# Attention scores in a fused attention and feed-forward kernel: q and k split into high and low parts, three float32r products per head pair in place of plain float32 tiles

## The chip, the cores and the metric

The kernel runs on one core of a Trainium2 chip. The metric is the device time of one launch in microseconds (us), as the median of several runs. TensorE (PE) does matrix products; its weight loads are listed as PEld. VectorE is DVE, ScalarE is ACT, GpSimd is POOL, and SyncE (SP) issues the DMAs. Each engine runs its own instructions in the order in which they were written.

## What is computed

```python
q, k, v: (4, 12, 448, 64); w_pre, w_post: (12, 12)
scores = scale * np.matmul(q, k.transpose(0, 1, 3, 2))
scores = np.einsum('bhij,hg->bgij', scores, w_pre)
scores = scores - np.max(scores, axis=-1, keepdims=True)
attn = np.exp(scores)
attn = attn / (np.sum(attn, axis=-1, keepdims=True) + 1e-09)
attn = np.einsum('bhij,hg->bgij', attn, w_post)
attn_out = np.matmul(attn, v)
# x: (4, 448, 768), the heads side by side
h = x.transpose(0, 2, 1) @ U @ V
u = x + h.transpose(0, 2, 1)
out = u + np.maximum(u @ w_ch1, 0.0) @ w_ch2      # 768 -> 3072 -> 768
```

All inputs and the output are float32.

## The kernel before

The work has three stages. In the first, attention runs over 16 units (4 batches, 4 groups of rows each) and 180 chunks of 10 rows. In the second, the products with w_ch1 run (`product`, L970), and in the third those with w_ch2 (`down`, L1078). Both of these use float32r operands that are kept as a high and a low part, with three products (low by high, high by low, high by high) summed in one bank.

The first stage goes through these steps.

- **Scores** (`qk`, L402 to L409): for each unit and each of 6 head pairs p, 96 times in all, four plain float32 products of 64 rows by 64 (or 60) columns. A pair's two heads lie in rows 0 to 63 and 64 to 127 of q and k; the 124 query columns are cut in two halves. One line of the program becomes two matrix instructions, so that a pair has 8.
- **Relay** (`qk_out` L411, `relay` L415): a copy of 124x896 from the bank to the tile s (three buffers), on ACT or DVE, and two DMAs from s to the tile t, which turn the layout round. The head mix needs all 12 relays of its unit.
- **Head mix and softmax**: `premix` (L440, 8 instructions), the maximum on DVE (L447), the exponentials on ACT (L452), `add_eps` on POOL (L455), the reciprocal on DVE (L458), `scale_w` on POOL (L462), and `postmix` (L476, 56 instructions). These two products too are of 64 rows by 64 columns.
- **Values** (`av`): 36 instructions at L517 of 128 rows by 64 columns, and 24 at L525 of 64 by 64. The path through U and V (L729, L746, L760) uses all 128 by 128.

The order is not left to a scheduler at compile time: `Plan` holds every step with a rank (the table `RANK`), engines it may run on with planned costs, and the slots of the buffers it needs, and plays the program through; what comes out is written to the engines in that order. Four PSUM tiles of two banks are shared by all steps.

Two more parts are touched. `narrow` turns float64 words of w_ch1, U and V into float32 with chains of DVE and POOL instructions; 11 such pieces ("early" ones) run within the first stage, through the raw tiles `kr`. At the start POOL sets parts of both t tiles to zero (L379).

Of the kernel before, what the change touches and what calls it, by code (L numbers as in the profile page):

```python
# [22 lines left out]
NG = 4  # L23
# [22 lines left out]
class Unit:  # L46
# [10 lines left out]
RANK = dict(  # L57
    e0=-75.527, estep=7.598, er=5.082, qk_lead=5.047, qk_step=0.838, av_off=4.137, av_step=0.9, post=4.408,
    kr=1.361, vr=0.943, qr=5.087, mx=0.654, ex=1.029, ep=2.968, po=2.286, qo=0.493, uv0=6, uvs=0.155, uv1=2.315,
    raw=5.531, k0=-13.668, kstep=0.83, m0=7.671, pu=1.842, ev=29.543, lead=14.78, t0=-2.958, ts=0.557, t1=2.815,  # L60
    ta=37.05, tb=3.706, dl=32.545, hl=13.674, out=3,
)
# [182 lines left out]
def build(tc, q2, kt, vj, wpre_in, wpost_in, u_in, v_in, ident, w1j, w2, out, show=None):  # L245
# [5 lines left out]
    def pool(ctx, name, bufs, side="left", **kw):  # L251
# [3 lines left out]
    BUFS = dict(  # L255
        wr=3, e=3, st=4, a0=1, a1=1, vr=1, kr=2, k=2, q=3, s=3, x=2, ea=1, xn=1, t3=1, hs=10, hr=5, b0=1, b1=1, b2=1,
    )
# [27 lines left out]
    pool(t0_ctx, "t0", 1)  # L285
    for n in ("kr", "x", "ea"):
        pool(whole, n, BUFS[n], "right")
    uT = [[None] * 7 for _ in range(2)]
# [8 lines left out]
    open_uT(0, 0)  # L297
    for n in ("k", "q", "s"):
        pool(qk_ctx, n, BUFS[n], "right")
# [89 lines left out]

    def load_k(eng, b, p, n):  # L390
        k = tile_of(("k", b), lambda: sb["k"].tile([128, H // 2, S], F32, "k", ("k", b)))
        eng.dma_start(out=k[:, p:p + n], in_=kt[b, :, p:p + n])

    def load_q(eng, u, p, n, src):
        q = tile_of(("q", u), lambda: sb["q"].tile([128, H // 2, QW], F32, "q", ("q", u)))
        eng.dma_start(out=q[:, p:p + n], in_=src[:, p:p + n])

    for b in range(B):
        for p, n in ((0, 1), (1, 2), (3, 3)):
            plan.add(("k", b, p), [("SP", (450, 1050 * n))], partial(load_k, b=b, p=p, n=n), rank_qk(b * NG, 2 * p) - RANK["kr"], (), [("k", b)])  # L400
# [18 lines left out]
    for u, un in enumerate(units):  # L419
        b, size = un.b, 128 * (H // 2) * QW  # L420
        src = q2[at:at + size].rearrange("(p h i) -> p h i", p=128, h=H // 2)
        at += size
        for p in range(0, H // 2, 3):
            plan.add(("q", u, p), [("SP", (430, 880))], partial(load_q, u=u, p=p, n=3, src=src), rank_qk(u, 2 * p) - RANK["qr"], (), [("q", u)])
        for p in range(H // 2):
            r = rank_qk(u, 2 * p)
            o, s = ("qk", (u, p)), ("s", (u, p))
            plan.add(("qk", u, p), [("PE", 760)], partial(qk, u=u, p=p), r, [("q", u, p // 3 * 3), ("k", b, (0, 1, 1, 3, 3, 3)[p])],
                     [o, ("q", u), ("k", b)])
# [134 lines left out]
    def open_qk(eng):  # L564
        qk_ctx.close()
        for j in range(1, 4):
            open_uT(0, j)
        open_aw(range(5))
# [64 lines left out]

    def raw_tile(key):
        return sb["kr"].tile([128, 2 * HW], F32, "kr", ("kr", key)).bitcast(I32).rearrange("p (n t) -> p n t", t=2)

    def narrow(key, src, n, p, rank, gate, home, hold=(), make=None):

        def load_raw(eng):
            T["raw", key] = raw_tile(key)[:p, :n]  # L640
            eng.dma_start(out=T["raw", key], in_=src)
# [34 lines left out]
        s = n / HW  # L676
        raw, x, hold = ("kr", key), ("x", key), list(hold)
        plan.add((key, 0), [("SP", (480, 1800 * s))], load_raw, rank - RANK["raw"], [gate], [raw])
# [19 lines left out]
    def direct(key, src, n, p, c, finish, cost):  # L698
        narrow(key, src, n, p, c + RANK["er"], ("premix", c // 2), partial(early_tile, key), [("ea", key)])
        for i in range(2):  # L700
# [194 lines left out]
    for F in range(NF):  # L895
# [4 lines left out]
        for i, f, h, j in pieces:  # L900
# [6 lines left out]
            g, re = early()  # L907
            narrow(key, src, HW, 128, re, g, partial(early_tile, key), [("ea", key)])
            done[i] = (key, "take")
# [265 lines left out]
```

## Time and profile before

| | us |
|---|---|
| median of 3 runs | 1049.65 (1046.68 to 1050.88) |
| profiled execution, whole time | 1046.06 |
| its span in the profile | 1044.3 |
| first head mix starts | 35.22 |
| last stage: products with w_ch2 | about 694 to 1042 |

The whole time of the profiled execution is 1.8 us over its span, and 3.6 us under the median. How to read it: the first 376 us are attention, in which all engines work and PE runs many kinds of products; after that PE runs one long row of equal products up to the end.

### The profile page before, as it was taken

The page shows a single profiled execution, that of the slowest core. Times are in us where ns is not written, and L with a number is a line of the kernel's source. Part 1 is how long each engine was busy: PE and PEld are TensorE (multiplying, and loading weights), DVE is VectorE, ACT ScalarE, POOL GpSimd, SP SyncE. Part 2 cuts the span into 40 slices and gives each one's busy share as a digit, 9 for nine tenths or more (in the row PEclk, how much of TensorE's full clock was granted, in tenths as well). Part 3 has the DMA queues.
Part 4 walks back from the last instruction along what each step waited for, and adds up shares of the span by engine and source line. Part 5 has one row for each costly group of instructions (what it writes and reads, how often), then busy time and mean ns, then how long its engine had stood idle before and what let it go on. Part 6 is the DMA issues. An engine that isn't in the chain of part 4 may idle for free.

```text
span 1044.3 us, 28592 instructions
## 1 busy us (share of the span) xinstructions
PE 998.9 (96%) x11908; PEld 837.0 (80%) x11908; DVE 782.5 (75%) x1175; ACT 474.9 (45%) x983; POOL 358.4 (34%) x462
## 2 busy tenths in 40 slices
PE   4798999999999998999999999999999999999998
PEld 1365766666666787899999999999999999999998
DVE  0474476468678779999999987894999999996323
ACT  2676767777777874443433333441333333420000
POOL 3122121123212576755555544450432423422000
PEclk8799999999999999999999999999999999999999
DMA  7556556466676324344444444686353454440023
GB/s 278 182 180 204 195 174 198 155 219 194 191 228 203 109 81 145 109 137 157 147 149 146 154 134 143 193 279 252 96 175 116 138 172 131 150 149 1 1 78 134
DMA packets 85345, 163.88 MB, mean 157 GB/s; under 512 B 8560, under 2 KB 69856, under 8 KB 84704
## 3 DMA queue, kind: packets, MB, share of 16 engines
q1 hardware_dynamic: 85216, 162.05, 48.0%
q8 instruction: 94, 1.54, 0.6%
q14 instruction: 35, 0.29, 0.1%
HBM read 86.13 MB, written 34.60 MB: 116 GB/s over the span
## 4 chain that ended last, share of the span: by engine, by line
PE 75%; DVE 13%; DMA 5%; ACT 3%; issue 2%; SPq 1%; POOL 0%; ACTq 0%; DVEq 0%
PE bank L1078 33%; PE bank L970 17%; PE bank L476 6%; PE bank L440 6%; PE bank L517 5%; PE bank L409 5%; DMA t<-s 3%; DVE aw L664 2%; DVE aw L665 2%; DVE x L670 2%; PE bank L525 1%; ACT e L452 1%; DVE aw L660 1%; DVE hs L983 1%; DVE x L669 1%
## 5 line engine op out<-in xcount | busy, mean ns | idle before, releaser
L1078 PE MATMUL bank<-u,w 128*128 128x448 f32 x1728 | 345.9, 362 | 0.0
L1078 PEld LDWEIGHTS bank<-u,w 128*128 128x128 f32 x1728 | 324.0, 188 | 21.6
L970 PE MATMUL bank<-u,w 128*128 128x448 f32 x1512 | 307.6, 364 | 3.9 <-DVE hs L983 3.0
L970 PEld LDWEIGHTS bank<-u,w 128*128 128x128 f32 x1512 | 283.3, 188 | 26.2 <-DVE hs L983 3.3
L1081 DVE TENSOR_TENSOR acc<-acc,bank 128x896 f32<-128x896 f32 (+1 forms) x99 | 104.3, 1053 | 79.3 <-PE bank L1078 79.0
L447 DVE TENSOR_REDUCE st<-bank 128x2 f32<-128x896 f32 x90 | 97.6, 1087 | 74.6 <-PE bank L440 65.0
L674 POOL TENSOR_TENSOR aw<-aw,x 128x384 f32<-128x384 f32 x70 | 79.2, 1131 | 203.1 <-DVE x L670 199.4
L476 PEld LDWEIGHTS bank<-wr,e 60*64 60x64 f32 x5040 | 91.1, 135 | 41.5 <-issue 29.9
L334 POOL TENSOR_TENSOR w<-aw,w 128x384 fp32r<-128x384 f32 x82 | 96.1, 1178 | 68.4 <-ACT w L327 67.0
L452 ACT ACTIVATE e<-bank,st 128x448 f32<-128x448 f32 x180 | 113.1, 639 | 11.2 <-DVE st L447 8.2
L327 ACT CAST w<-aw 128x384 fp32r<-128x384 f32 x99 | 50.3, 514 | 138.7 <-PE bank L1078 67.2
L409 PE MATMUL bank<-k,q 64*64 64x448 f32 (+1 forms) x768 | 96.6, 571 | 16.6 <-ACT s L327 9.7
L653 ACT ACTIVATE x<-kr 128x384 f32<-128x384 f32 (+1 forms) x81 | 45.0, 555 | 136.2 <-DMA kr<-in_w 101.0
L476 PE MATMUL bank<-wr,e 60*64 60x60 f32 x5040 | 94.5, 219 | 7.7 <-issue 6.8
L440 PE MATMUL bank<-t,wpre 64*64 64x448 f32 x720 | 89.3, 557 | 10.0 <-DMA t<-s 7.1
L455 POOL TENSOR_SCALAR st<-st 128x2 f32<-128x2 f32 x90 | 18.8, 209 | 199.4 <-ACT e L452 198.2
L327 ACT COPY s<-bank 124x896 f32<-124x896 f32 x71 | 64.4, 911 | 40.5 <-DMA t<-s 21.6
L327 ACT COPY hs<-bank 128x448 f32<-128x448 f32 x88 | 46.8, 533 | 65.2 <-PE bank L970 59.6
L665 DVE SCALAR_TENSOR_TENSOR aw<-x,aw 128x384 f32<-128x384 f32 x88 | 69.8, 793 | 6.7
L1038 DVE SCALAR_TENSOR_TENSOR u<-hs,u 128x448 fp32r<-128x448 f32 x96 | 74.5, 807 | 0.0
L327 ACT COPY a<-bank 128x840 f32<-128x840 f32 (+1 forms) x67 | 56.2, 843 | 36.5 <-PE bank L476 36.2
L670 DVE SCALAR_TENSOR_TENSOR x<-kr,x 128x384 f32<-128x384 uint32 (+2 forms) x99 | 66.7, 674 | 3.4
(68 smaller groups left out, 1011.6 us busy)
## 6 DMA issues: line engine op xcount, KB each, us to landing
t<-s SPq DMA_DIRECT2D x192, 210.0 KB
hd<-hs SPq DMA_DIRECT2D x96, 224.0 KB
hs<-hd SPq DMA_DIRECT2D x96, 224.0 KB
kr<-in_w1j SPq DMA_DIRECT2D x48, 384.0 KB
kr<-in_w SPq DMA_DIRECT2D x48, 384.0 KB
v<-in_vj SPq DMA_DIRECT2D x4, 1536.0 KB
q<-in_q SPq DMA_DIRECT2D x32, 186.0 KB
ud<-acc SPq DMA_DIRECT2D x12, 448.0 KB
```

The lines of the kernel that those rows point to most:

```text
L327: eng.copy(out=o, in_=i)
L334: eng.tensor_tensor(out=o, in0=a, in1=b, op=ALU.subtract)
L409: eng.matmul(o[at, i, :S], lhsT=q[d, p, at], rhs=k[d, p, :], start=True, stop=True)
L440: eng.matmul(o[64 * j:64 * j + 64, i, :S], lhsT=wpre[64 * i:min(64 * i + 64, QW)], rhs=tt[u % 2][64 * i:min(64 * i + 64, QW), n, :], start ...
L447: eng.tensor_reduce(out=mx, in_=T["pre", k][:, :, :S], axis=AX.X, op=ALU.max, negate=True)
L452: eng.activation(out=e[:, i], in_=T["pre", k][:, i, :S], func=ACTF.Exp, bias=T["mx", k][:, i:i + 1], accum_out=sm[:, i:i + 1])
L476: eng.matmul(d, lhsT=e[64 * j:64 * j + HALF, i, x * KB:x * KB + KB], rhs=wr[64 * j:64 * j + HALF, i].rearrange("p (g m) -> p g m", m=MH), ...
L665: eng.scalar_tensor_tensor(out=f32(a), in0=f32(x), scalar=MIN_NORMAL, in1=f32(a), op0=ALU.is_ge, op1=ALU.mult)
L670: eng.scalar_tensor_tensor(out=f32(x), in0=raw[:, :, 0].bitcast(U32), scalar=2.0**-52, in1=f32(x), op0=ALU.mult, op1=ALU.mult)
L970: eng.matmul(o, lhsT=w[:, x, i * 128:(i + 1) * 128], rhs=u[:, i, y, :], start=j < 2 and i + t == 0, stop=i + t == 4, skip_group_check=True)
L1078: eng.matmul(ps[:, j, :S], lhsT=w[:, x, cc * 128:(cc + 1) * 128], rhs=h, start=(i == 0), stop=(i == len(todo) - 1))
L1081: eng.tensor_tensor(out=two(b, c, n), in0=two(b, c, n), in1=T.pop(("dn", g, b, c))[:, :n, :S], op=ADD)
```

## The change

The tiles of q and k become float32r tiles with a high and a low part. For each half of a unit's q (three head pairs) and for each head pair of a batch's k, `split_in` adds a DMA to a staging tile (`qs`, `ks`, or the tiles a0 and a1, which are free at the start), a copy that rounds to the high part, and a subtraction that gives the low part. `qk` then does three products of 64 rows by 124 columns for each of the two heads (6 instructions for a pair). k is held in 6 slots, one for each head pair, in place of two whole batches; q in 3 half units in place of 3 units. The early pieces of `narrow` get a raw ring `ke` of their own with one buffer, the ring `kr` is opened only after the scores, and the numbers of `RANK` are others. The order in which the scores are done is fixed by `plan.lines`.

```diff
-    e0=-75.527, estep=7.598, er=5.082, qk_lead=5.047, qk_step=0.838, av_off=4.137, av_step=0.9, post=4.408,
-    kr=1.361, vr=0.943, qr=5.087, mx=0.654, ex=1.029, ep=2.968, po=2.286, qo=0.493, uv0=6, uvs=0.155, uv1=2.315,
+    e0=-109.606, estep=13.112, er=5.066, qk_lead=5.047, qk_step=0.848, av_off=4.58, av_step=1.123, post=4.44,
+    kr=1.39, vr=0.771, qr=4.691, mx=0.76, ex=0.868, ep=3.004, po=2.297, qo=0.455, uv0=7.863, uvs=-0.133,
...
+    STAGE = {("k", 0): "a1", ("q", 0): "a0"}
...
+    def split_in(n, u, p, width, src, shape, slot, rank):
+        held, at = stage(n, u, p, width)
...
+        def high(eng):
+            T[n, u, p] = sb[n].tile(shape, F32R, n, slot)
+            copy(eng, part(0), raw())
+
+        def low(eng):
+            sub(eng, part(1), raw(), f32(part(0)))
...
+        plan.add((n, u, p, "raw"), [("SP", (450, 2.35 * width))], fetch, rank - RANK["inn"], (), [held])
+        plan.add((n, u, p, "h"), HIGH(width), high, rank, [(n, u, p, "raw")], [held, slot], port=BOTH)
+        plan.add((n, u, p, "l"), LOW(width), low, rank, [(n, u, p, "h")], [held, slot], port=BOTH)
...
     def qk(eng, u, p):
-        q, k = T["q", u], T["k", units[u].b]
+        q, k = T["q", u, p // 3], T["k", units[u].b, p]
         o = T["qk", u, p] = bank("qk", (u, p))
-        for j in range(2):
-            at = slice(64 * j, min(64 * j + 64, QW))
+        for n, (x, y) in enumerate(((1, 0), (0, 1), (0, 0))):
             for i in range(2):
                 d = slice(i * D, (i + 1) * D)
-                eng.matmul(o[at, i, :S], lhsT=q[d, p, at], rhs=k[d, p, :], start=True, stop=True)
+                eng.matmul(o[:QW, i, :S], lhsT=q[d, p % 3, x, :], rhs=k[d, y, :], start=n == 0, stop=n == 2)
...
-    after("open_qk", open_qk, [("relay", nu - 1, h) for h in range(H)])
+    after("open_qk", open_qk, [("relay", nu - 1, h) for h in range(H)] + [(("w", F, i), "put") for F in range(2) for i in (0, 1, 3, 4)])
...
+    plan.lines = [[(n, u, p) for u in range(nu) for p in range(H // 2)] for n in ("qk", "qk_out")]
```

PE, in the middle of attention, before (L440 is the head mix, L409 the scores, L476 the second head mix; the shape is that of the output):

```order
L440 MATMUL bank3_61<-t1_143,wpre_141 64x448 x4
L476 MATMUL bank1_59<-wr_2_334,e_2_290 64x12x5 x24
L476 MATMUL bank1_59<-wr_2_334,e_2_290 64x60 x4
L409 MATMUL bank2_60<-k_0_151,q_0_149 64x448 x2
L409 MATMUL bank2_60<-k_0_151,q_0_149 60x448 x2
L440 MATMUL bank0_58<-t1_143,wpre_141 64x448 x4
L476 MATMUL bank1_59<-wr_0_288,e_0_260 64x12x5 x24
```

PE at a like place of the changed kernel (L465 is the head mix, L435 the scores, L501 the second head mix):

```order
L465 MATMUL bank3_61<-t1_149,wpre_147 64x448 x4
L501 MATMUL bank2_60<-wr_0_331,e_0_313 64x12x5 x24
L501 MATMUL bank2_60<-wr_0_331,e_0_313 64x60 x4
L435 MATMUL bank1_59<-k_1_182,q_0_165 124x448 x6
L465 MATMUL bank0_58<-t0_148,wpre_147 64x448 x4
L435 MATMUL bank2_60<-k_2_184,q_0_165 124x448 x6
L501 MATMUL bank1_59<-wr_1_367,e_1_319 64x12x5 x24
```

The score rows go from 64 columns to 124, between neighbours of 64 columns that stay as they were. Over the whole program, places where the next product uses another cut of rows and columns than the one before go from 115 to 253; the first 10 head pairs stand in one run in both kernels.

POOL in the first microseconds, before (the two t tiles set to zero, then the softmax):

```order
L379 MEMSET t0_142 4x5376
L379 MEMSET t1_143 4x5376
L455 ISA
L455 TENSOR_SCALAR st_0_250<-st_0_250 128x2
L462 TENSOR_TENSOR wr_0_288<-wpost_144,st_0_250 128x120
```

POOL there in the changed kernel (L333 is the subtraction that gives a low part):

```order
L378 MEMSET t0_148 4x5376
L378 MEMSET t1_149 4x5376
L333 ISA
L333 TENSOR_TENSOR k_0_176<-a_0_158,k_0_176 128x448
L333 TENSOR_TENSOR k_2_184<-a_0_158,k_2_184 128x448
L333 TENSOR_TENSOR k_4_188<-a_0_158,k_4_188 128x448
L333 TENSOR_TENSOR q_2_193<-qs_0_172,q_2_193 128x3x124
L333 TENSOR_TENSOR q_1_170<-qs_0_172,q_1_170 128x3x124
```

The low part of the first k now stands behind both memsets. Over the whole program POOL gets 53 of the new copies and subtractions (26 and 27), DVE 29 subtractions, ACT 30 copies.

POOL later in attention, in the changed kernel (L480 is add_eps, L487 scale_w, L330 the copy to a high part):

```order
L487 TENSOR_TENSOR wr_0_331<-wpost_150,st_1_311 128x120
L330 TENSOR_SCALAR k_0_176<-ks_0_179 128x448
L333 TENSOR_TENSOR k_0_176<-ks_0_179,k_0_176 128x448
L480 TENSOR_SCALAR st_2_317<-st_2_317 128x2
L487 TENSOR_TENSOR wr_1_367<-wpost_150,st_2_317 128x120
L330 TENSOR_SCALAR q_0_165<-qs_0_172 128x3x124
L480 TENSOR_SCALAR st_3_382<-st_3_382 128x2
L333 TENSOR_TENSOR q_0_165<-qs_0_172,q_0_165 128x3x124
L487 TENSOR_TENSOR wr_2_424<-wpost_150,st_3_382 128x120
```

The new instructions stand between the softmax steps, which before had POOL to themselves but for the early pieces.

SP, in the first microseconds, issues before the first relay: before, one unit's q and a batch's k, then q of two further units, v, and all of the second batch's k (5.5 MB in all); in the changed kernel the first unit's q and the first k, half a unit's q, v and one sixth of the second k (3.8 MB).

## Rows read from the trace of the kernel before

**Rows 1.** The page: busy time of each engine, share of the span, instructions.

```profile
PE 998.9 (96%) x11908; PEld 837.0 (80%) x11908; DVE 782.5 (75%) x1175; ACT 474.9 (45%) x983; POOL 358.4 (34%) x462
```

**Rows 2.** Busy time by stage: stretch, length, engines, clock share, DMA share, GB/s.

```profile
0.00:40.00 40.00, 17.93 (x116) 5.09 (x120) 2.63 (x3) 12.34 (x17) 9.47 (x7) 0.74 0.73 247
40.00:376.00 336.00, 322.34 (x8409) 218.33 (x8401) 226.00 (x366) 249.47 (x552) 88.59 (x218) 0.99 0.58 181
```

**Rows 3.** PE in order of time, 140 to 154 us: start, length, instructions.

```profile
140.41 0.74 PE L746 MATMUL bank<-xl,u 112*128 112x256 f32 x4
140.99 0.64 PE L746 MATMUL bank<-xh,u 112*128 112x256 f32 x4
141.56 0.98 PE L440 MATMUL bank<-t,wpre 64*64 64x448 f32 x8
...
144.82 0.67 PE L760 MATMUL bank<-v,t 128*128 128x448 f32 x2
145.42 1.04 PE L476 MATMUL bank<-wr,e 60*64 60x60 f32 x56
146.29 0.93 PE L409 MATMUL bank<-k,q 64*64 64x448 f32 x8
147.04 0.93 PE L440 MATMUL bank<-t,wpre 64*64 64x448 f32 x8
147.79 0.93 PE L409 MATMUL bank<-k,q 64*64 64x448 f32 x8
148.55 0.99 PE L476 MATMUL bank<-wr,e 60*64 60x60 f32 x56
149.47 1.92 PE L517 MATMUL bank<-a,v 128*64 128x110 f32 x36
...
152.47 0.99 PE L476 MATMUL bank<-wr,e 60*64 60x60 f32 x56
153.28 0.93 PE L409 MATMUL bank<-k,q 64*64 64x448 f32 x8
```

**Rows 4.** PE in order of time, 393 us: all neighbours use 128 by 128.

```profile
393.13 0.64 PE L746 MATMUL bank<-xl,u 112*128 112x256 f32 x4
393.62 0.63 PE L746 MATMUL bank<-xh,u 112*128 112x256 f32 x4
394.09 1.98 PE L970 MATMUL bank<-u,w 128*128 128x448 f32 x9
```

**Rows 5.** Busy time of the engines in 20 us of the last stage.

```profile
720.00:740.00 20.00, 20.00 (x102) 18.75 (x101) 14.05 (x19) 4.25 (x8) 4.33 (x5) 1.00 0.16 54
```

**Rows 6.** POOL's first long instructions, in order of time.

```profile
0.72 9.08 POOL L379 MEMSET t<- 4x5376 f32 x2 [0.29 <-POOLq L1163]
```

**Rows 7.** The chain that ended last, from the start to the first head mix.

```profile
10.34 0.94 SPq L416
11.32 10.08 DMA t<-s
21.56 0.91 ACT s L327
23.30 5.22 DMA t<-s
30.36 4.85 DMA t<-s
35.22 3.87 PE bank L440 x24
```

**Rows 8.** Groups of instructions by shape: busy time, mean ns, idle before and what ended it.

```profile
L334 POOL TENSOR_TENSOR u<-acc,u 128x448 fp32r<-128x448 f32 x25 | 31.4, 1274 | 9.1 <-ACT u L327 7.3 <-PE bank L729 1.5
L331 POOL TENSOR_SCALAR u<-acc 128x448 fp32r<-128x448 f32 x5 | 3.0, 603 | 0.2
L334 DVE TENSOR_TENSOR u<-acc,u 128x448 fp32r<-128x448 f32 x14 | 14.9, 1074 | 2.6 <-ACT u L327 2.5
```

**Rows 9.** Waits of PE's weight loads, 40 to 376 us: total, times, longest.

```profile
PEld bank L476 <- POOL wr L462: 8.1, 23, 0.9
```

More of the change, by code (lines that the diff above doesn't have):

```diff
@@ L255, in build @@
     BUFS = dict(
[L256 removed]
+        wr=3, e=3, st=4, a0=1, a1=1, vr=1, kr=2, k=6, q=3, ks=1, qs=1, s=3, x=2, ke=1, ea=1, xn=1, t3=1, hs=10, hr=5, b0=1, b1=1, b2=1,
     )
@@ L285, in build @@
     pool(t0_ctx, "t0", 1)
-    for n in ("kr", "x", "ea"):
-        pool(whole, n, BUFS[n], "right")
+    pool(whole, "x", BUFS["x"], "right")
     uT = [[None] * 7 for _ in range(2)]
@@ L297, in build @@
     open_uT(0, 0)
-    for n in ("k", "q", "s"):
+    for n in ("ke", "ea", "k", "q", "ks", "qs", "s"):
         pool(qk_ctx, n, BUFS[n], "right")
@@ L388, in rank_av, with stage @@
         return first[u + 1] + RANK["av_off"] + p * RANK["av_step"]
[L390 to L396, printed above, removed]
+    STAGE = {("k", 0): "a1", ("q", 0): "a0"}
+    def stage(n, u, p, width):
+        if (n, u) not in STAGE:
+            return (n + "s", (u, p)), lambda: sb[n + "s"].tile([128, width], F32, n + "s", (n + "s", (u, p)))
+        home = STAGE[n, u]
+        whole_a = (home, "stage")
+        return whole_a, lambda: sb[home].tile([128, XA, 120], F32, "a", whole_a).rearrange("p x t -> p (x t)")[:, p * width:(p + 1) * width]
@@ new lines, in split_in, with fetch, part, raw @@
+    def split_in(n, u, p, width, src, shape, slot, rank):
+        held, at = stage(n, u, p, width)
+        def fetch(eng):
+            T[n, u, p, "raw"] = at()
+            o = T[n, u, p, "raw"]
+            eng.dma_start(out=o if n == "k" else o.rearrange("p (h i) -> p h i", i=QW), in_=src)
+        def high(eng):
[3 more added lines that the diff above has]
+            sub(eng, part(1), raw(), f32(part(0)))
+        def part(x):
+            return T[n, u, p][:, x] if n == "k" else T[n, u, p][:, :, x]
+        def raw():
+            o = T[n, u, p, "raw"]
+            return o if n == "k" else o.rearrange("p (h i) -> p h i", i=QW)
+        plan.add((n, u, p, "raw"), [("SP", (450, 2.35 * width))], fetch, rank - RANK["inn"], (), [held])
+        plan.add((n, u, p, "h"), HIGH(width), high, rank, [(n, u, p, "raw")], [held, slot], port=BOTH)
+        plan.add((n, u, p, "l"), LOW(width), low, rank, [(n, u, p, "h")], [held, slot], port=BOTH)
@@ L422, in build @@
         at += size
-        for p in range(0, H // 2, 3):
-            plan.add(("q", u, p), [("SP", (430, 880))], partial(load_q, u=u, p=p, n=3, src=src), rank_qk(u, 2 * p) - RANK["qr"], (), [("q", u)])
+        for i in range(2):
+            split_in("q", u, i, 3 * QW, src[:, 3 * i:3 * i + 3], [128, 3, 2, QW], ("q", (u, i)), rank_qk(u, 6 * i) - RANK["qr"])
         for p in range(H // 2):
@@ L565, in open_qk @@
         qk_ctx.close()
+        pool(whole, "kr", BUFS["kr"], "right")
         for j in range(1, 4):
@@ L632, in build, with raw_tile, narrow @@
     after("open_tail", open_tail, ["open_a"] + [("av", nu - 1, p) for p in (0, AV)])
-    def raw_tile(key):
-        return sb["kr"].tile([128, 2 * HW], F32, "kr", ("kr", key)).bitcast(I32).rearrange("p (n t) -> p n t", t=2)
-    def narrow(key, src, n, p, rank, gate, home, hold=(), make=None):
+    def raw_tile(ring, key):
+        return sb[ring].tile([128, 2 * HW], F32, ring, (ring, key)).bitcast(I32).rearrange("p (n t) -> p n t", t=2)
+    def narrow(key, src, n, p, rank, gate, home, hold=(), make=None, ring="kr"):
         def load_raw(eng):
-            T["raw", key] = raw_tile(key)[:p, :n]
+            T["raw", key] = raw_tile(ring, key)[:p, :n]
             eng.dma_start(out=T["raw", key], in_=src)
@@ L676, in narrow @@
         s = n / HW
-        raw, x, hold = ("kr", key), ("x", key), list(hold)
+        raw, x, hold = (ring, key), ("x", key), list(hold)
         plan.add((key, 0), [("SP", (480, 1800 * s))], load_raw, rank - RANK["raw"], [gate], [raw])
@@ L698, in direct @@
     def direct(key, src, n, p, c, finish, cost):
-        narrow(key, src, n, p, c + RANK["er"], ("premix", c // 2), partial(early_tile, key), [("ea", key)])
+        narrow(key, src, n, p, c + RANK["er"], ("premix", c // 2), partial(early_tile, key), [("ea", key)], ring="ke")
         for i in range(2):
@@ L907, in build @@
             g, re = early()
-            narrow(key, src, HW, 128, re, g, partial(early_tile, key), [("ea", key)])
+            narrow(key, src, HW, 128, re, g, partial(early_tile, key), [("ea", key)], ring="ke")
             done[i] = (key, "take")
```

11 lines of the change are left out of this document (5 added, 6 removed).

## The prediction

> **What bounds the kernel now.** I read the page first: PE is busy for 96% of the span [rows 1]. The busy time by stage then says where a change to the scores can count. From 40 to 376 us, the attention stage behind its start, PE is busy for 322.3 of 336 us, ACT for 249, DVE for 226 and POOL for 89 [rows 2]; in the late products PE has no gap at all, 20.00 of 20 us [rows 5]. So what PE gains or loses in attention moves the end nearly one to one, and the last two stages, which do the same work in both kernels, only follow. In the first 40 us PE is busy for 18 us alone: the chain of waits lies there on the relays t<-s, which land at 21.4, 28.5 and 35.2 us, and the first head mix starts at 35.22 us [rows 7]. The start is a part with its own bound, DMA.
>
> **What a head pair's scores cost before.** PE in order of time gives the distance from one start to the next: 146.29 to 147.04 and 147.79 to 148.55, so 0.755 us for a pair [rows 3]. That holds where the next product has the same cut of 64 rows by 64 columns. L476 shows what a change of cut costs. Its 56 instructions take 0.81 us where L409 follows (152.47 to 153.28), and 0.92 us where L517 follows, with 128 rows (148.55 to 149.47): 0.11 us for leaving the cut. Behind L760, of 128 by 128, the same 56 take 0.87 us (145.42 to 146.29): 0.06 us for coming back. And a float32r product of 128 columns pays for both its ends: the 8 of L746 take 1.15 us between 64 by 64 neighbours (140.41 to 141.56) [rows 3], and 0.96 us among neighbours of their own cut (393.13 to 394.09) [rows 4]: 0.19 us. An excursion from 64 by 64 to wide float32r products and back costs 0.11 + 0.19 + 0.06 = 0.36 us by these rows.
>
> **The new scores.** A pair becomes three steps of two products, one for each head, in different rows of the array. A float32r step of 448 columns takes 20.00 / 102 = 0.196 us [rows 5]. The four tiles of a score product ran side by side before (8 instructions in 0.755 us, [rows 3]), so I take the two row halves to do the same: 3 x 0.196 = 0.588 us. No row shows two float32r products side by side; the bounds are 0.588 us and, one after the other, 6 x 0.196 = 1.176 us. I take the lower, since rows of the same array and the same 64 row halves show it. The Trainium skill, "TensorE: Matmul & The Clock Gate", Part 3, says that products in distinct row groups run concurrently, but gives 3.07 in place of 4 for four of them; at that efficiency the three steps would be an estimated 0.77 us and their gain gone, and no row here shows that loss.
>
> Saved: 0.755 - 0.588 = 0.167 us a pair. Of 96 pairs the first 10 stand ahead of the first head mix, where PE waits anyway; 86 x 0.167 = 14.4 us.
>
> Added: the scores now have 64 rows by 124 columns, between neighbours of 64 by 64. The order has 115 changes of cut before and 253 after, 138 more, which is 69 excursions. Whether going from 64 to 124 columns at 64 rows is such a change, no row shows: all changes in the trace alter the rows, or go to or from 128 rows. The bounds are nothing and 0.36 us; I take 0.36, because each pair of different cuts in the trace pays and none is free. 69 x 0.36 = 24.8 us. The Trainium skill says it outright, in "TensorEngine Tiling (Array Packing)", Key Properties: changing the tiling mode, not just the tile, drains TensorE. By that rule the sum on PE is +10.4 us, by the reading that only rows matter -14.4 us; the trace agrees with the rule wherever it has a case.
>
> Net on PE: 24.8 - 14.4 = +10.4 us. PE is busy 96% of the stage, so a small part falls into gaps: **+10.0 us**.
>
> **The splits.** 53 new instructions on POOL, 29 on DVE, 30 on ACT. By the nearest rows a copy on POOL is 0.60 us, a subtraction 1.27 us, and on DVE 1.07 us [rows 8]: 26 x 0.60 + 27 x 1.27 = 50 us more on POOL, whose 89 us [rows 2] become about 139 of 336; 29 x 1.07 = 31 us on DVE, some 257 of 336; ACT, at a copy's 0.60 us, has 18 us more, 267 of 336. None becomes the bound; the idle time of each hides them. What they cost is lateness. The softmax goes over POOL twice (L455, L462), and the new instructions stand in that queue between the two; behind them waits postmix, and behind that all of PE. Before, PE's weight loads waited for POOL's L462 for 8.1 us in all [rows 9]. If that grows with POOL's busy time, by 139 / 89, it is 12.7 us: **+4 us**, rounded down because some of the splits lie in the start. The bounds are 0, if every split falls into a gap, and +10, if each of the 53 holds up its chain by 0.2 us.
>
> **The start.** POOL has its memsets until 9.80 us [rows 6], and the low part of the first k stands behind them: 9.80 + 1.27 [rows 8], then a score pair at the lower of the clock's two levels, 1.2 GHz (the stretch has 0.74 of the full clock, [rows 2]), twice 0.588 or 1.2 us, and a copy of 0.91 us [rows 7]; the first relay can be issued at about 13.2 us, not at 10.34 [rows 7]. Yet before it landed only at 21.40 us, behind 5.5 MB; now 3.8 MB are ahead. At 247 GB/s [rows 2] that is 7.0 us less. The first pair should land at about 13.2 + 5.2 = 18.4 us (5.22 us is a later relay's way, [rows 7]), up to 3 us earlier, and the two further rounds of 7 us each, in a queue without the second k, give back another us or so. **-4 us**; bounds 0 and -7.0.
>
> **The rest.** The early pieces of narrow run in one raw buffer instead of two but are spread (steps of 13.1 chunks where there were 7.6); a chunk is about 336 / 180 = 1.9 us, so a piece has 25 us for its load and chain. I take nothing; the cover is that distance, and if it failed, the ring kr would open late, at the gate open_qk. 12 more loads of q and k lie in SP's queue behind relays, hidden by their lead of 2.6 chunks, 5 us.
>
> **Sum.** 10.0 + 4 - 4 = +10 us. On the profiled execution, 1046.1, that gives 1056; the median of the runs lies 3.6 us over it, so 1049.65 + 10, or **1059.5 us**.
>
> **The rivals.** *No drain for columns alone* (0.17). If 64 by 64 and 64 by 124 count as one mode, the 69 excursions are free and only the saving is left: -14.4 x 0.96 - 4 + 4 = -13.8, so 1036 us. It speaks for it that no row has this pair; against it that no change of cut in the trace is free. It decides below 14.4 / 69 = 0.21 us an excursion.
>
> *Splits too late* (0.13). k's parts are made only 1.39 chunks, 2.6 us, ahead of their use, and a copy and a subtraction on POOL need 1.9 us of that. If each of the 18 later k parts and 30 later q halves holds PE up by 0.25 us, that is 12 us more: 1071 us.
>
> *Row halves one after the other* (0.05): 1.176 - 0.755 = 0.42 us more a pair, 86 x 0.42 + 24.8 = 61 us: about 1111 us. The four tiles that ran side by side speak against it.
>
> *The terms cancel* (0.08): the drains fall into waits of PE that are there already and the start gives its full 7 us; 1050 us, no change.
>
> My forecast has the remaining 0.57; its own range is 1051 to 1068 us, from the bounds of start and splits.
>
> **How the numbers follow.** A change under 0.5% (5 us) can't be told from none here. Of my case three quarters lie above 1055, the rest within; with the late splits and the serial halves that makes 0.6 slower. Same is 0.2, from the low side of my case and the cancelling. Faster is 0.2, nearly all the free change of cut. The range from 1036 to 1072 leaves out the serial halves, and half of the free change and of the late splits: 0.2.
>
> **What would show it.** In the changed trace: a score group of 6 should take 0.78 to 0.82 us to the next start, not 0.6, with its first product about 0.1 us longer than the rest; L501 should take 0.92 us ahead of L435 and 0.81 ahead of L465. Two products of a step should start within some ns. The first head mix should start near 31 us. PE's busy time from there to the end of attention should grow by about 10 us, and waits for POOL's L487 to about 12 us. If L501 takes 0.81 us ahead of the scores, my main term is wrong and the kernel is faster; if the start is at 35 us or later, or the head mixes wait for score parts, the time is over 1065.

## The result, and the profile after

| | before | changed |
|---|---|---|
| median | 1047.07 (1043.73 to 1056.87, 20 runs) | 1055.34 (1049.52 to 1062.27, 20 runs) |
| profiled execution, whole time | 1046.06 | 1052.03 |
| its span | 1044.3 | 1050.2 |

The ratio is 1.0069, 95% interval 1.0046 to 1.0093: the changed kernel is slower by 7.2 us (0.0069 x 1047), 4.8 to 9.7 us. Forecast were +10 us and 1059.5 us; of the 4.2 us between 1059.5 and 1055.34, 2.6 come from the median before, which was 1049.65 over three runs and is 1047.07 over twenty. The executions of one kernel spread over 13 us here, so what is said below of a few us goes by ratios; a single trace serves for durations, orders and large differences.

The page of the changed kernel answers to [rows 1]: PE is busy 4.4 us longer in the whole program.

```profile
span 1050.2 us, 28363 instructions
...
PE 1003.3 (96%) x11716; PEld 855.2 (81%) x11716; DVE 802.0 (76%) x1205; ACT 493.4 (47%) x1016; POOL 405.6 (39%) x511
```

By stage, as in [rows 2]:

```profile
0.00:40.00 40.00, 19.87 (x224) 11.73 (x224) 12.36 (x16) 21.40 (x37) 17.28 (x19) 0.83 0.65 216
40.00:376.00 336.00, 320.88 (x8041) 226.24 (x8034) 234.13 (x383) 254.87 (x558) 122.72 (x254) 1.00 0.60 188
```

From 40 to 376 us PE is not busier than before (320.9 and 322.3 us), and yet the work got less far: the last product of the second head mix starts at 378.1 us instead of 373.8. POOL, DVE and ACT are busier by 34, 8 and 5 us; none comes near the stage's 336.

A fixed stretch that PE nearly fills in both kernels can't show how much more work PE has. Between the same two points of the work, from the start of the first head mix to the end of the last second head mix, it can be seen (before, then changed):

```profile
35.22:374.02 338.80, 325.14 (x8431) 218.57 (x8431) 226.92 (x365) 250.75 (x554) 88.08 (x219) 0.99 0.58 182
29.55:378.27 348.72, 332.73 (x8259) 232.62 (x8259) 242.14 (x392) 263.25 (x576) 128.28 (x263) 0.99 0.60 187
```

Here PE is busy for 7.6 us more, where the forecast had about 10; its pauses go from 13.7 to 16.0 us, and the stretch is 9.9 us longer, of which the earlier first head mix takes back 5.7. In this one pair of traces the forecast's large terms look nearly right. But busy time has a spread of its own: e9 below, with the instructions of the kernel before, is busy for 329.0 us between these two points. It takes the experiments to tell.

PE in order of time, the same columns as [rows 3]:

```profile
152.31 0.88 PE L435 MATMUL bank<-k,q 64*124 64x448 f32 x6
153.12 0.98 PE L465 MATMUL bank<-t,wpre 64*64 64x448 f32 x8
153.92 0.99 PE L501 MATMUL bank<-wr,e 60*64 60x60 f32 x56
154.84 0.87 PE L435 MATMUL bank<-k,q 64*124 64x448 f32 x6
155.64 0.98 PE L465 MATMUL bank<-t,wpre 64*64 64x448 f32 x8
156.55 0.87 PE L435 MATMUL bank<-k,q 64*124 64x448 f32 x6
157.35 1.04 PE L501 MATMUL bank<-wr,e 60*64 60x60 f32 x56
158.22 0.94 PE L465 MATMUL bank<-t,wpre 64*64 64x448 f32 x8
159.08 0.87 PE L435 MATMUL bank<-k,q 64*124 64x448 f32 x6
```

Every price of the change of cut can be read here as the distance of two starts. A pair's scores take 0.81 us (152.31 to 153.12) or 0.80. The 56 of L501 take 0.92 us ahead of the scores (153.92 to 154.84) and 0.87 behind them (157.35 to 158.22). The head mix, 0.755 us where all around has its cut, takes 0.80 us behind scores (153.12 to 153.92), 0.86 ahead of them (158.22 to 159.08) and 0.91 with scores on both sides (155.64 to 156.55). So leaving costs 0.11 us, coming back 0.05, and the group itself 0.21 over the 0.588 of its three steps: 0.37 us an excursion. What PE loses so at a change of cut is called a drain below. In the records of single instructions the two row halves of a step start 4 ns apart, and a group's first product takes 463 ns where the later ones take 363.

The start, in order of time (all engines; to be held against [rows 6, 7]):

```profile
9.86 3.71 POOL L333 TENSOR_TENSOR k<-a,k 128x448 fp32r<-128x448 f32 x3
...
11.03 5.72 PE L435 MATMUL bank<-k,q 64*124 64x448 f32 x40 [4.20 <-POOL k L333]
12.18 0.91 ACT L326 COPY s<-bank 124x896 f32<-124x896 f32 x1 [1.76 <-PE bank L435]
13.11 5.11 SPq L442 DMA_DIRECT2D t<-s  x6
...
29.55 4.76 PE L465 MATMUL bank<-t,wpre 64*64 64x448 f32 x24 [3.38 <-DMA t<-s]
```

The first low part of k does stand behind the memsets, the first relay is issued at 13.11 us (forecast 13.2), and the first head mix starts at 29.55 us, 5.7 us earlier than before (forecast 31).

The splits, groups by shape as in [rows 8], and the wait of [rows 9]:

```profile
L333 POOL TENSOR_TENSOR k<-ks,k 128x448 fp32r<-128x448 f32 x12 | 13.7, 1140 | 3.8 <-ACT k L326 3.3
L333 POOL TENSOR_TENSOR q<-qs,q 128x372 fp32r<-128x372 f32 x12 | 11.8, 980 | 17.6 <-ACT q L326 17.0
L330 POOL TENSOR_SCALAR q<-qs 128x372 fp32r<-128x372 f32 x18 | 9.1, 503 | 34.8 <-PE bank L435 25.0 <-DMA qs<-in_q 9.4
```

```profile
PEld bank L501 <- POOL wr L487: 8.1, 14, 1.4
```

The durations are somewhat below the forecast's (1.14 and 0.98 us for a subtraction, where 1.27 was taken, and 0.50 for a copy, where 0.60 was). In the whole program POOL is busy for 47 us more (forecast 50), DVE for 19.5 (forecast 31) and ACT for 18.5 (forecast 18). In this trace the wait for POOL's scale_w has not grown: 8.1 us, as before, not 12.7.

### The profile page after: what moved, and what is told of

Read it like the earlier page. It is cut to its first block, busy times and chain, and to the rows that moved or that the text cites. A ratio compares the mean times of both kernels' runs of the same rounds, so it can differ in the third digit from the quotient of the medians.

```text
span 1050.2 us, 28363 instructions
## 1 busy us (share of the span) xinstructions
PE 1003.3 (96%) x11716; PEld 855.2 (81%) x11716; DVE 802.0 (76%) x1205; ACT 493.4 (47%) x1016; POOL 405.6 (39%) x511
## 3 DMA queue, kind: packets, MB, share of 16 engines
q8 instruction: 92, 1.51, 0.6%
## 4 chain that ended last, share of the span: by engine, by line
PE 84%; DMA 5%; DVE 4%; ACT 3%; issue 2%; SPq 1%; POOL 1%; ACTq 0%; DVEq 0%; POOLq 0%
PE bank L1104 33%; PE bank L996 27%; PE bank L501 6%; PE bank L542 6%; PE bank L435 5%; PE bank L465 4%; DMA t<-s 4%; PE bank L550 1%; DVE st L472 1%; ACT s L326 1%; ACT e L477 1%; SPq L442 1%; PE bank L772 1%; PE bank L755 1%; DMA a<-in_kt 0%
## 5 line engine op out<-in xcount | busy, mean ns | idle before, releaser
L333 POOL TENSOR_TENSOR w<-aw,w 128x384 fp32r<-128x384 f32 x84 | 98.2, 1175 | 64.2 <-ACT w L326 62.9
L501 PEld LDWEIGHTS bank<-wr,e 60*64 60x64 f32 x5040 | 85.5, 135 | 40.3 <-issue 24.7
L326 ACT CAST w<-aw 128x384 fp32r<-128x384 f32 x103 | 52.6, 516 | 132.2 <-PE bank L1104 67.3
L679 ACT ACTIVATE x<-kr 128x384 f32<-128x384 f32 x78 | 43.3, 556 | 135.4 <-DMA kr<-in_w 101.0
L501 PE MATMUL bank<-wr,e 60*64 60x60 f32 x5040 | 93.2, 220 | 8.2 <-issue 3.1
L435 PE MATMUL bank<-k,q 64*124 64x448 f32 x576 | 83.7, 403 | 17.5 <-ACT k L326 6.1
L465 PE MATMUL bank<-t,wpre 64*64 64x448 f32 x720 | 87.3, 564 | 5.4 <-DMA t<-s 3.4
L435 PEld LDWEIGHTS bank<-k,q 64*124 64x124 f32 x576 | 48.8, 189 | 50.7 <-ACT e L477 9.6
L326 ACT COPY s<-bank 124x896 f32<-124x896 f32 x79 | 71.5, 910 | 36.4 <-DMA t<-s 15.4
L1060 ACT ACTIVATE u<-hs 128x448 fp32r<-128x448 f32 x96 | 54.4, 579 | 26.3 <-DMA hs<-hd 25.4
L542 PE MATMUL bank<-a,v 128*64 128x120 f32 (+3 forms) x1152 | 63.0, 263 | 3.8 <-issue 1.9
```

What stands on the lines that cost most here:

```text
L326: eng.copy(out=o, in_=i)
L333: eng.tensor_tensor(out=o, in0=a, in1=b, op=ALU.subtract)
L435: eng.matmul(o[:QW, i, :S], lhsT=q[d, p % 3, x, :], rhs=k[d, y, :], start=n == 0, stop=n == 2)
L465: eng.matmul(o[64 * j:64 * j + 64, i, :S], lhsT=wpre[64 * i:min(64 * i + 64, QW)], rhs=tt[u % 2][64 * i:min(64 * i + 64, QW), n, :], start ...
L501: eng.matmul(d, lhsT=e[64 * j:64 * j + HALF, i, x * KB:x * KB + KB], rhs=wr[64 * j:64 * j + HALF, i].rearrange("p (g m) -> p g m", m=MH), ...
L542: eng.matmul(main[i * D:(i + 1) * D, c, :n], lhsT=v[:, p + c, i, x, :], rhs=a[:, x * H + 2 * (p + c) + i, :n], start=(c == 0 and x == 0), ...
```

## The experiments

All were timed in five rounds beside the kernel before on the same chip; ratios are to that kernel, and a difference in us is that of two ratios times 1047, good to 3 to 5 us. The changed kernel was not timed again in these rounds; its ratio is that of the first table. The first seven ask which part of the change costs what, the last five what sets the pace of attention in the changed kernel's order. In the last five, theory A is the prediction's step (PE's work moves the end nearly one to one), B that the order with its waits sets the length, C that the softmax chain does, D that loading instructions does.

**No change of cut: e1_bf16_cut64.** The changed kernel in its own order, with the parts held as bfloat16, so that the twelve products (three for each of the old four tiles) keep the old cut. The parts carry fewer bits than float32r's.

```diff
-            T[n, u, p] = sb[n].tile(shape, F32R, n, slot)
+            T[n, u, p] = sb[n].tile(shape, BF16, n, slot)
...
-                eng.matmul(o[:QW, i, :S], lhsT=q[d, p % 3, x, :], rhs=k[d, y, :], start=n == 0, stop=n == 2)
+            for j in range(2):
+                at = slice(64 * j, min(64 * j + 64, QW))
+                for i in range(2):
+                    d = slice(i * D, (i + 1) * D)
+                    eng.matmul(o[at, i, :S], lhsT=q[d, p % 3, x, at], rhs=k[d, y, :], start=n == 0, stop=n == 2)
```

> The changed kernel in its own order, with the parts in bfloat16 in place of float32r (the scores carry fewer bits) and twelve products of 64 rows by 64 or 60 columns in place of six of 64 by 124, so that the scores have the same cut as their neighbours. Theory A (the changes of cut cost the time): the 69 excursions of 0.36 us go away, 24.8 x 0.96 = 24 us: about 1031 us, under both kernels; a score group takes 0.57 to 0.60 us to the next start, and L501 ahead of it 0.81 us instead of 0.92. Theory B (splits and new order cost it, the changes of cut fall into waits that are there anyway): 1053 to 1055 us.

Measured: 1052.18 us, ratio 1.0039 (1.0018 to 1.0060), 3 us less than the changed kernel. Its PE in order of time, and the stage's busy times:

```profile
151.51 0.99 PE L504 MATMUL bank<-wr,e 60*64 60x60 f32 x56
152.32 0.75 PE L438 MATMUL bank<-k,q 64*64 64x448 bf16 x12
152.89 0.93 PE L468 MATMUL bank<-t,wpre 64*64 64x448 f32 x8
153.64 0.99 PE L504 MATMUL bank<-wr,e 60*64 60x60 f32 x56
```

```profile
40.00:376.00 336.00, 307.88 (x8548) 221.76 (x8541) 234.21 (x383) 253.85 (x559) 120.78 (x256) 0.99 0.62 189
```

The drains are gone: 0.81 us ahead of the scores (151.51 to 152.32), 0.57 for a pair (152.32 to 152.89), 0.75 for the head mix behind it. PE is busy for 13 us less in the stage (320.9 to 307.9), and of that 3 us reach the end (0 to 6, by the two intervals). This is where the prediction's reading fails.

**Only the wide cut: e2_wide_plain.** The kernel before, in its own order, with plain float32 products of 124 columns instead of 64 and 60.

```diff
-        for j in range(2):
-            at = slice(64 * j, min(64 * j + 64, QW))
-            for i in range(2):
-                d = slice(i * D, (i + 1) * D)
-                eng.matmul(o[at, i, :S], lhsT=q[d, p, at], rhs=k[d, p, :], start=True, stop=True)
+        for i in range(2):
+            d = slice(i * D, (i + 1) * D)
+            eng.matmul(o[:QW, i, :S], lhsT=q[d, p], rhs=k[d, p, :], start=True, stop=True)
```

> The kernel before with plain float32 scores in two products of 64 rows by 124 columns in place of four of 64 by 64 or 60; nothing else, no splits, the same order. Theory A: the streaming time stays 0.75 us a pair, but some 77 excursions into another cut come in at 0.31 us (0.11 for leaving, 0.05 for the first weights of plain float32, 0.09 for leaving again, 0.06 for coming back), 24 x 0.96 = 23 us: about 1070 us. Theory B: 1047 us, as before.

Measured: 1058.41 us, ratio 1.0097 (1.0070 to 1.0124), +10 us.

```profile
158.69 0.99 PE L474 MATMUL bank<-wr,e 60*64 60x60 f32 x56
159.62 1.02 PE L407 MATMUL bank<-k,q 64*124 64x448 f32 x4
160.56 0.98 PE L438 MATMUL bank<-t,wpre 64*64 64x448 f32 x8
```

0.93 us ahead of the scores and 0.94 for a pair: the drain is that of columns alone, without float32r and without splits. PE is busy 1019.4 us in the whole program, 20.5 more than in [rows 1]; half of it reaches the end (7 to 13 us).

**The order alone, first try: e3_order_alone.** The changed kernel's table and loads, without splits, plain products. The planner plays the program through, and without the splits the load itself held the slot; what it wrote was not the changed kernel's order, the path through U and V came late in it.

> The changed kernel's order, start and buffers, but without copies and subtractions (the DMA writes the plain float32 tile) and with the four plain float32 products of before. Theory A: the order costs nothing and the earlier first head mix gives its 5.7 us: 1041 to 1043 us. Theory B: the order with its shallower buffers is the loss: 1050 us or more.

Measured: 1070.3 us, ratio 1.0220 (1.0189 to 1.0252). It doesn't answer its question. It shows only that another order of the same work, with fewer tiles for q and k than in e6 below, costs 20 us more than e6.

**Splits without the new products: e5_splits_old_products,** in the changed kernel's order. The old four tiles, from the high part of q and the low part of k alone.

```diff
+        for j in range(2):
+            at = slice(64 * j, min(64 * j + 64, QW))
...
-                eng.matmul(o[:QW, i, :S], lhsT=q[d, p % 3, x, :], rhs=k[d, y, :], start=n == 0, stop=n == 2)
+                eng.matmul(o[at, i, :S], lhsT=f32(q[d, p % 3, 0, at]), rhs=f32(k[d, 1, :]), start=True, stop=True)
```

> The changed kernel with all its copies and subtractions, but the four plain float32 products of before, cut 64 by 64 (the scores are the high part of q by the low part of k alone). Theory A: PE has 10 us less than in the changed kernel, 1045 us, and the distance to the order alone is the price of the splits, some 4 us. Theory B: the splits come late and cost most of it: 1053 us or more.

Measured: 1053.26 us, ratio 1.0053 (1.0024 to 1.0083). The stage's busy times:

```profile
40.00:376.00 336.00, 312.50 (x8054) 208.68 (x8046) 229.10 (x375) 249.41 (x549) 116.58 (x247) 0.99 0.60 185
```

**Neither: e6_no_splits.** The changed kernel's order to the letter, the loads writing plain tiles (12 for k and 6 half units of q, more than the changed kernel has), no copies and no subtractions, the old four tiles.

```diff
-            copy(eng, part(0), raw())
+            pass
...
-            sub(eng, part(1), raw(), f32(part(0)))
+            pass
```

> The changed kernel's order on every engine, exactly, but with no copies and subtractions (the loads write plain float32 tiles of which there are enough, 12 for k and 6 half units for q) and the four plain float32 products of before. Against e5 it shows the splits alone, against the kernel before the order and the start alone. Theory A (PE's work sets the time): PE's work is that of before and the start is 5.7 us earlier, 1042 us. Theory C (in the changed kernel something other than PE sets the pace, and drains fall into its waits): if that is the splits and their single staging buffers, 1042 to 1046 us; if it is the order itself, 1050 us or more.

Measured: 1049.33 us, ratio 1.0016 (0.9983 to 1.0049). Its first head mix starts at 28.5 us. So the ladder, from the kernel before over e6 and e5 to the changed kernel, is: order and start +1.7 us, splits +3.9 (with what their fewer tiles cost), new products +1.7. Each step alone is within its uncertainty of nothing; that the products cost 10 us is not. In e5 PE is idle for 23.5 of the 336 us, in the changed kernel for 15.1, as if what the wide cut added went into pauses; but the kept execution of e5 is 3.4 us longer than that of the changed kernel, though its ratio is the lower one, so that a good part of these 8 us is chance. PE's wait for POOL's scale_w is 6.2 us in e6's trace and 14.3 in e5's.

**Deeper buffers: e7_bf16_deep.** e1 with five tiles s instead of three, and three staging tiles for k and q each.

```diff
-        s = T["s", u, p] = sb["s"].tile([QW, 2, S], F32, "s", ("s", (u, p)))
+        s = T["s", u, p] = sb["s"].tile([QW, 2, S], F32, f"s{(u * (H // 2) + p) % 5}")
```

> e1 (bfloat16 parts, cut 64 by 64) in the same order on every engine, with the room that the smaller parts leave used for more buffers: five tiles s instead of three, three staging tiles each for q and k instead of one. Theory C, with the relays and the loads that wait for these buffers in SP's queue as the pace: 1036 to 1043 us, and the relays and loads leave the chain that ended last. If the buffers are not it: 1052 us, as e1.

Measured: 1049.93 us, ratio 1.0016 (0.9990 to 1.0041), 2 us less than e1 and not told apart from it. The 9 to 16 us that were expected if these buffers set the pace are excluded.

**The early start alone: e9_late_k.** The kernel before, with the second batch's k loaded behind the first unit's last relay.

```diff
+    late = [x for x in order if x[0][0] == "k" and x[0][1] == 1]
+    order = [x for x in order if x not in late]
+    to = [x[0] for x in order].index(("relay", 0, H - 1)) + 1
+    order[to:to] = late
```

> The kernel before, with the three loads of the second batch's k (1.4 MB) moved in SP's queue from ahead of the first relay to behind the first unit's last relay; nothing else. If the bytes ahead of the relays set the start: 1.4 MB at 247 GB/s, 5.5 us, first head mix near 30 us and 1042 us in all. If the relays are bound by their own ring of three buffers: first head mix at 35 us, 1047 us.

Measured: 1049.55 us, ratio 1.0010 (0.9981 to 1.0039). The first head mix comes at 29.8 us, 5.4 earlier than before. An eighth of the second head mixes is reached at 72.1 us (before 73.8), a quarter at 115.6 (before 115.4): in this trace the gain is given back within 90 us, in the order of before too.

**A third of the products: s1_one_step.** The scores of the changed kernel from one step, low by low, instead of three.

```diff
-        for n, (x, y) in enumerate(((1, 0), (0, 1), (0, 0))):
+        for n, (x, y) in enumerate(((1, 1),)):
...
-                eng.matmul(o[:QW, i, :S], lhsT=q[d, p % 3, x, :], rhs=k[d, y, :], start=n == 0, stop=n == 2)
+                eng.matmul(o[:QW, i, :S], lhsT=q[d, p % 3, x, :], rhs=k[d, y, :], start=True, stop=True)
```

> The changed kernel in its own order, with one product step for each pair of heads instead of three: the scores come from the low parts of q and k alone, so the output differs by that. Splits, loads, excursions to the 64x124 cut and all else stay; 96 groups lose four of their six matmuls, about 0.39 us each by the steps of 0.2 us in the trace of the changed kernel, so TensorE has some 37 us less to do in the attention stage. Theory A, TensorE's work moves the end nearly one to one (0.96, the step of the prediction): about 1055 - 36 = 1019 us. Theory B, what sets the attention stage's length is the order with its waits, and work taken off TensorE turns into idle time there, as the runs with bfloat16 parts showed with 0.13 of 24 us: about 1050 us, with the pauses of TensorE between 40 and 376 us grown by some 30 us.

Measured: 1045.17 us, ratio 0.9966 (0.9933 to 0.9999), 11 us less than the changed kernel. The page's busy times, and those of the stage:

```profile
PE 974.2 (93%) x11332; PEld 829.1 (79%) x11332; DVE 799.6 (76%) x1205; ACT 491.9 (47%) x1016; POOL 403.7 (38%) x511
```

```profile
40.00:376.00 336.00, 294.81 (x7653) 202.90 (x7656) 231.53 (x380) 252.69 (x555) 120.09 (x253) 0.99 0.60 186
```

PE is busy 29 us less, and idle for 41 of the 336 us; this execution took 1052.26 us, 7 us over the median of its kernel, and some of that idle time will be its own. Theory A (1019 us) falls; B had 1050, and the time lies 5 us under it.

**Half the exponentials: s2_half_exp.**

```diff
-        eng.activation(out=e[:, i], in_=T["pre", k][:, i, :S], func=ACTF.Exp, bias=T["mx", k][:, i:i + 1], accum_out=sm[:, i:i + 1])
+        eng.activation(out=e[:, i, :S // 2], in_=T["pre", k][:, i, :S // 2], func=ACTF.Exp, bias=T["mx", k][:, i:i + 1], accum_out=sm[:, i:i + 1])
...
-                eng.matmul(d, lhsT=e[64 * j:64 * j + HALF, i, x * KB:x * KB + KB], rhs=wr[64 * j:64 * j + HALF, i].rearrange("p (g m) -> p g m", m=MH),
+                eng.matmul(d, lhsT=e[64 * j:64 * j + HALF, i, x % 3 * KB:x % 3 * KB + KB], rhs=wr[64 * j:64 * j + HALF, i].rearrange("p (g m) -> p g m", m=MH),
```

> The changed kernel in its own order, with the exponentials over the first half of the 448 columns alone; the second head mix reads those columns twice, so sums and weights are of half the keys. ScalarE has about 180 x 0.3 = 54 us less to do in the attention stage, nothing else changes. If ScalarE's exponentials (theory C: the softmax chain is what the heads' mixes wait for) set the stage's pace, the time falls by 15 us or more, to 1040 or below. If they lie beside TensorE's work (theories A and B), 1050 to 1055 us.

Measured: 1055.56 us, ratio 1.0064 (1.0028 to 1.0100). ACT is busy 461.7 us, 32 less than in the changed kernel (the estimate of 54 was too high), and the time is the same.

**Half the maximum: s3_half_max.**

```diff
-        eng.tensor_reduce(out=mx, in_=T["pre", k][:, :, :S], axis=AX.X, op=ALU.max, negate=True)
+        eng.tensor_reduce(out=mx, in_=T["pre", k][:, :, :S // 2], axis=AX.X, op=ALU.max, negate=True)
```

> The changed kernel in its own order, with the row maximum taken over the first half of the columns alone (the values after the softmax stay the same in exact arithmetic, since the maximum is only subtracted). VectorE has about 90 x 0.54 = 49 us less to do in the attention stage. If VectorE's place in the chain from the first mix to the second sets the pace (theory C), 1040 us or below; if not (A and B), 1050 to 1055 us.

Measured: 1058.5 us, ratio 1.0075 (1.0037 to 1.0113). DVE is busy 762.7 us, 39 less, and the time is the same. Theory C falls for the changed kernel.

**All three: s5_all_three,** s1 with the edits of s2 and s3.

> One product step in three, the exponentials over half the columns and the maximum over half the columns, together, in the changed kernel's order: the scores come from the low parts alone and the sums and weights are of half the keys. With one step alone TensorE's work fell by 29 us and the time by 11: TensorE's pauses grew by 24 us, of which stops inside a group of equal products, with nothing named as releaser, were 7 and waits for other engines and transfers, ScalarE above all, 17. If the softmax chain on ScalarE and VectorE took what TensorE gave (theory C, after TensorE has been made shorter), shortening it too now gives the rest: 10 us or more below the run with one step, about 1033 us, with the waits for ScalarE back at the changed kernel's 4 to 6 us. If what took it is the supply of TensorE's instructions and the transfers (theory D and the score copies' relay), neither is shorter here: 1040 to 1047 us, with stops of 13 us or more.

Measured: 1043.2 us, ratio 0.9954 (0.9920 to 0.9989), not told apart from s1. So the softmax on ACT and DVE isn't what took PE's gain in s1 either. The stops that theory D expected are not there in this trace (4.2 us in all, against 12.9 in that of s1, each one execution): the time fits D, the stops don't.

**Twice the instructions: s4_twice_instr.** e1 with each product written as two of 224 columns.

```diff
-                for i in range(2):
+                for i, c in ((0, 0), (1, 0), (0, 1), (1, 1)):
...
-                    eng.matmul(o[at, i, :S], lhsT=q[d, p % 3, x, at], rhs=k[d, y, :], start=n == 0, stop=n == 2)
+                    cols = slice(c * S // 2, (c + 1) * S // 2)
+                    eng.matmul(o[at, i, cols], lhsT=q[d, p % 3, x, at], rhs=k[d, y, cols], start=n == 0 and c == 0, stop=n == 2, skip_group_check=True)
```

> The kernel with bfloat16 parts in the 64x64 cut, each of its products written as two matmuls of 224 columns instead of one of 448: the same columns stream, but there are 1152 x 2 more... that is 24 matmuls a pair instead of 12, some 2300 more instructions with their weight loads in the whole kernel. It asks whether the number of TensorE's instructions is part of the pace: in the traces TensorE stops for 1 to 4 us inside a group of equal products just when a transfer of instructions (16 KB packets) runs on its own DMA queue. If loading instructions counts (theory D), 5 to 10 us more than the kernel with 12 products, about 1058 us; if only the columns streamed count (A), the same 1052 us; if the fixed part of each matmul shows on TensorE but goes into pauses that are there anyway (B), also about 1052 us with TensorE busier.

Measured: 1070.25 us, ratio 1.0197 (1.0150 to 1.0245), 16.5 us more than e1. Where nothing stops them, a pair's 24 products take 0.57 us (146.19 to 146.76 below), as the 12 did, so it is not that each product got dearer. In order of time, and then PE's waits in the stage, total, times and longest, in this kernel and (last fence) in e1:

```profile
146.19 0.78 PE L439 MATMUL bank<-k,q 64*64 64x224 bf16 x24
146.76 1.02 PE L505 MATMUL bank<-wr,e 60*64 60x60 f32 x56
```

```profile
PE bank L505 <- issue: 19.4, 16, 3.2
PE bank L439 <- issue: 5.5, 9, 0.9
```

```profile
PE bank L504 <- issue: 7.5, 6, 2.5
PE bank L504 <- ACT s L327: 2.8, 2, 2.0
```

"issue" is a stop inside a group for which the profile names no releaser. Over all lines from 40 to 380 us they are 26.9 us here and 8.2 in e1: 18.7 us more, about as much as the loss, though not the loss itself: between the first head mix and the last second head mix PE's pauses of all kinds grow by 12.6 us and its busy time by 6.6. Theory D, which had 5 to 10 us, holds for this kernel; the last section shows what the stops are. They are no part of what the changed kernel lost: in its trace they are 5.0 us, in that of the kernel before 7.3.

## Why the prediction was right, and which steps were not

**The drain: right, and shown.** The doubtful question was whether 64 by 64 and 64 by 124 count as different cuts. They do: L501 takes 0.92 us ahead of L435, and 0.81 in e1, in the same order, where the cut stays. e2 shows it without float32r. The excursion costs 0.37 us (forecast 0.36), the pair 0.80 (forecast 0.78 to 0.82), and the two row halves run together. That removes the rivals of the free change of cut and of the serial halves. The Trainium skill, "TensorEngine Tiling (Array Packing)", Key Properties, has the drain as a rule for a change of the tiling mode; these rows agree with it and give the price for columns alone. That the drains are what made the changed kernel slower is not shown: in the order of before the wide cut alone costs 10 us (e2), but in the changed order the new products with their drains cost 1.7 us (4 either way), and no step of the ladder alone is told from nothing.

**"What PE gains or loses in attention moves the end nearly one to one": wrong.** This is the step that failed, and with it the term of +10.0 us, which by the ladder is +1.7 (4 either way). Changes of PE's busy time in the whole program, and what reached the end (busy time is good to some 5 us: s2 and s3, with the changed kernel's products, have 1005.5 and 1008.6 where it has 1003.3):

| | PE busy | time |
|---|---|---|
| e2 against before | +20.5 | +10.2 |
| e1 against changed | -14.4 | -3.1 |
| s1 against changed | -29.1 | -10.8 |

The share is between 0.2 and 0.5, and with the uncertainty of both columns it stays under 0.9, where the prediction took 0.96. Between the first head mix and the last second head mix, PE's busy time and pauses can be read in e2, e1 and s1 as in the first section (length, then PE's busy time):

```profile
33.13:384.52 351.39, 345.63 (x8087) 219.32 (x8087) 227.18 (x365) 252.85 (x554) 87.87 (x219) 0.99 0.56 176
29.80:377.03 347.23, 317.85 (x8775) 227.35 (x8775) 241.08 (x392) 261.64 (x576) 124.53 (x263) 0.98 0.61 188
29.41:379.74 350.33, 307.46 (x7915) 210.18 (x7915) 241.47 (x392) 262.54 (x576) 126.94 (x263) 0.99 0.60 186
```

In e2 the pauses fall from the 13.7 us of before to 5.8, in e1 they rise from the changed kernel's 16.0 to 29.4, in s1 to 42.9. A busy share of 96% left 14 us of pauses in the stage before, and the prediction took these as all that could absorb; but busy and idle time trade. The reading that fits, argued and not tested by itself: PE runs its rows in a fixed order, and many rows wait for a copy, a relay or a softmax that comes at its own time; work added ahead of such a wait shortens the wait (e2), work taken away lengthens it (e1, s1). What then holds the changed order at its length is not ACT's exponentials or DVE's maximum: half the exponentials, half the maximum and both with a third of the products move nothing beyond what the products alone do. Which mix of relays, copies out of the banks and stops it is stays open. Nor do the drains add up on PE: 69 excursions of 0.37 us less 14.4 are 11.1 us, but PE's busy time is only 2.9 us over e5's between the first head mix and the last second head mix, and 7.6 over that of before. The rival of the cancelling terms had the right mechanism, drains that fall into waits, and too low a time, since it counted on the start's 7 us.

**The splits, +4 us: right in size as far as it can be told** (+3.9, give or take 5, from e6 to e5), and the way it was put is neither shown nor excluded. PE's wait for scale_w, forecast to grow to 12.7 us, is 8.1 in the changed kernel's trace as in that of before, but 14.3 in e5's against 6.2 in e6's, the pair that differs by the splits. The rival of the late splits, which asked for 12 us more, is excluded.

**The start, -4 us: wrong.** The mechanism was right and the gain larger than forecast (5.7 us at the first head mix), but e9, with 5.4 us of it, shows that it is not kept: the end moves by +1.0 us (-2.0 to +4.1). What the late rows wait for instead was not followed.

**The sum** came out near (+7.2 for +10) by luck: two terms were too large with opposite signs, the drains by 8 us, the start by 4 or more. Its range is slightly off: the bounds of start and splits give 1052.7 to 1069.7, not 1051 to 1068; the measured time lies in both. The edits costed at nothing (narrow's ring, the further loads) lie in e6 with the order, +1.7 us (-1.8 to +5.1): nothing that can be told.

## What to carry to other kernels

Price a change of cut from the distances of starts in the trace, for columns alone too; here that came within 0.01 us. But don't multiply it by the busy share of an engine that runs in order between others: ask by a kernel with work taken away how much of a microsecond reaches the end (here 0.2 to 0.5, roughly), before a product is made faster there. And count instructions beside columns: many short products can be slowed by their own loading.

## What the hardware showed that was not expected

**PE stops to load its instructions.** The page lists DMA queues by packets, MB and share; q8 carries instructions. The changed kernel, then s4:

```profile
q8 instruction: 92, 1.51, 0.6%
```

```profile
PE 995.4 (93%) x13444; PEld 874.8 (82%) x13444; DVE 802.2 (75%) x1205; ACT 491.9 (46%) x1016; POOL 401.9 (38%) x511
...
q8 instruction: 106, 1.74, 0.7%
```

A packet is 16 KB (1.51 MB / 92). The packets follow PE's matmuls and weight loads: 92 for 2 x 11716 = 23432 instructions, 106 for 2 x 13444 = 26888, in s1 89 for 22664, so one packet for about 255. In none of the fourteen traces do two of them begin less than 3.29 us apart in attention. The 56 matmuls and 56 weight loads of a second head mix, though, run through in 0.81 us, which would empty a packet in 1.8 us. PE in order of time in s4, and the DMA in a short window just ahead:

```profile
168.05 0.93 PE L505 MATMUL bank<-wr,e 60*64 60x60 f32 x49
172.13 0.48 PE L505 MATMUL bank<-wr,e 60*64 60x60 f32 x7 [3.15 <-issue]
```

```profile
q1 hardware_dynamic: 113, 0.24, 73.1%
q8 instruction: 1, 0.02, 4.9%
```

The window is 169.6 to 170.8 us: the packet begins at 169.7, among bulk transfers that take 73% of the engines' time, 6.5 us after the one before it, and PE goes on 2.4 us later. Of the 22 stops of over 0.5 us within equal products of s4, 19 end 2.2 to 2.8 us after a packet begins; the packets begin 4.4 us apart there at the median, so that chance would put some 3 of the 22 in that stretch. The kernel before has it too:

```profile
180.01 1.03 PE L476 MATMUL bank<-wr,e 60*64 60x60 f32 x54
184.28 0.32 PE L476 MATMUL bank<-wr,e 60*64 60x60 f32 x2 [3.24 <-issue]
```

Its packet begins 2.6 us ahead of 184.28. These times and s4's cost show the stops to be loads; why some packets come late was not tried.

**Work taken away, little to show.** Three engines of one stage could each be relieved of 29 to 39 us (PE by s1, ACT by s2, DVE by s3) with 11, 0 and 0 us to show for it.
